# A longer spin, output weights staged in layer two's key buffers, and a new instruction order in a two-layer recurrent-memory transformer kernel

## The chip, the cores and the metric

The kernel runs on one core of one Trainium2 chip. The metric is the device time of one execution in microseconds (us), lower is better; the median of several executions is used. A profiled execution gives, beside its time, the span from its first to its last instruction and a trace of every instruction.

The core's engines work side by side, each through its own queue in order: PE (TensorE, matrix products), PEld (its weight loads), ACT (ScalarE), DVE (VectorE), POOL (GpSimd) and SP, which here mainly issues DMAs. Matrix products write to eight banks of PSUM (psC0, psC1, psG0 to psG5); ACT or DVE then copies the result to SBUF, which is called an eviction below.

## The reference

Two blocks are applied twice to x, a sequence of 2,048 tokens of 448 values. Block A is attention over segments of 32 tokens with a recurrent memory of 8 rows; block B is a gated MLP. Cut to what matters:

```python
def A(x, mem0, Wq, Wk, Wv, Wo):            # 16 heads of 256
    mem = mem0
    for s in range(64):
        h = concatenate([mem, x[32 * s : 32 * s + 32]])       # 8 + 32 rows
        q, k, v = h @ Wq, h @ Wk, h @ Wv                      # per head
        scores = (q @ k.T) / 16     # masked: the 32 rows causally, the 8 memory rows see all
        o = softmax(scores) @ v
        o = o @ Wo                                            # summed over heads
        mem = o[:8]; outs.append(o[8:])
    return concatenate(outs)

def B(x, Wg, Wu, Wd):                       # 448 -> 1792 -> 448
    return (relu(x @ Wg) * (x @ Wu)) @ Wd

x = x + A(layernorm(x));  x = x + B(layernorm(x))
x = x + A(layernorm(x));  x = x + B(layernorm(x))             # the same weights again
```

The memory makes block A a chain: segment s needs the memory rows that segment s - 1 gave.

## The kernel before, in words

**Weights.** The kernel first folds the weights. For each head it makes a product of Wq and Wk (tensor `A`, 16 heads in pairs) and a product of Wv and Wo (tensor `Bsb`), so that a layer needs only `u = h A`, scores `u h^T`, `y = P h` and `o = y B`. `weights()` loads Wq and Wk of four groups of pairs into staging slots `Wst` (which lie in `Bsb`), turns each half by eight transposes on PE (`transposes`, matmuls at L818), evicts them to `WT` (in `glu`), and multiplies (`product`, matmuls at L832). Wv and Wo are staged as well: Wo of eight pairs lies in two pieces of `glu`, three of `P3`, two of `Ug` and one of `GG`. `values(0)` and `values(1)` turn Wv and multiply by Wo into `Bsb`, four pairs each. A buffer that serves as staging is written for its real purpose only when the last product has read it; `s.alias` and the lists `homes` and `held` make these dependences.

**The first loads.** The first group's Wq and Wk come in eight half loads on SP (192 KB each) and four tails of 64 rows on ACT's queue; the other groups in whole loads with tails. All DMAs of SP go out in SP's order.

**The chain.** `chain(step)` does one segment's memory rows for both layers at once; layer two runs `LAG = 7` steps behind layer one. A step goes: u of 16 rows (matmuls at L1008, in two halves), eviction to `Usb`, transposes on DVE (`turn_u`), scores (L1204), softmax, y (L1262, L1265), o against all of `Bsb` (L1047), then a split into a high and a low part, a small product with `Sel`, and copies to `mT`, to `HT` (POOL, L1080) and to `HR`. The first two steps use the unfolded Wv and Wo (`unfused`, L1113 to L1136). `mT` is what the next step starts from.

**The bulk.** `att_group(l, t, g, bo)` does the 32-token rows of tile t (128 tokens) in layer l for a quarter of the heads: u (L1350, two PE steps), scores (L1376), softmax, y, and o (matmuls at L493). `glu_units` and `glu_down` do block B (L1453 for two tiles at once, L1482 for one). Layer norms are in `norm()`.

**Buffers the change touches.** `HT[l][i]` holds the transposed rows of a tile (tokens and memory), `HR[l][i][p]` the same rows as they stand; layer two has three of each (`NB = (2, 3)`). `Ug[0]` and `Ug[1]` hold an attention group's u. A part of `Ug` must be zero, and `values(1)` clears it when Wo has been read from there.

**The order.** All operations are recorded with their dependences in `_Sched`. A planner with fixed costs then sets each engine's order, with one exception: the order of PE is given by hand, as the string `LINE` (which operation comes next, as a place in the list of those left). The string `ORDER` shifts the priority of the units for the other engines. Where the plan has PE idle for over 300 ns, a `filler` is put in (matmuls at L1518 whose result nobody reads). At run time each engine goes through its own list and waits only on semaphores, so PE never overtakes a waiting instruction.

**The spin.** Ahead of everything PE runs matmuls on zeros (L726), to have been busy before the first weights arrive.

**Tilings.** The array is used whole (128x128), or in two tiles of 64x128, two of 128x64, four of 128x32 or eight of 64x32, by the operands' shapes.

Of the kernel before, what the change touches and what calls it, by code (L numbers as in the profile page):

```python
# [12 lines left out]
D = 448  # L13
H = 16
# [4 lines left out]
L = SEG + M  # L19
# [13 lines left out]
ORDER = ("nxaaaaRsTJCzqNVMHniXRBAAODOorIenAPcbGLePMZTGQySGNMXZBDwVyuXhaACIHMfFCXuphjeYMKYtUsaWkfMXtpJaAgHaAbLaADAaaifqaa"  # L33
         "CaErvaIxqaWGwaRkhOaaLuqWkNdgaQuPXZBKEynmeoJu0HfCQl0MwaaatbabtAkiXHsQsZ0dHowILewNSoxIZjcHVaNeDjCfCagAauEXqApt0j"
         "TRxJQkadZnDmoUpHkKAFrefyXxZyAfa0AaCuLCodjnUCwiPsJMumVy0TMpAFSpzPpN0YWHTHGtFqFRlusRAfoMzlZSXZNuHXUKaU0a00bqjuDu"
         "cFNcqkuriahKqgGDnmKHXCPHllFMUmAPOcnzgFaLsaadbMEbHAzMlqUalEZAZizDQgaACUlydMwOKrjOTlLTvA0jvRyfduychiEayenUPAKOBB"
         "IBcapvaNSwmHpHBiFqvwgFrd0XhGXvIpPtWuIbMdReygmGGJvVtwMaAoaNGALx0XHI0UoMSEEkSachUGKI0JuLiFEcwQpAbsmYtqbUupfRABfN"
         "ze0r0rTHlxXSarXfBOaiHaijfdEcucmPIzmyBaNgyigcQXRJEIqSDxNLXsuRdOOfOfYaaO0atzGjqhbmuGEHrcNyUgojwyQYJCiksNHhdXJQcY"
         "YOWSocVtAeQVNmadnRfxwyWGqcEMsNsvHaEQaNUOQV0CqJHn0tGCeaapxJaAVqQfjPuPDDlOg0NsVmlUorZaAwauSIJuThQdIMZFYGMKxZzIwI"
         "nHKpgwgRCWBXCgzBgcavLyLLkxnD0UQjvcZaZpTYcDPwacUQaUKaupymeEQhiBhplfCdH0CDklUQEALrUmDmVsArfamfjdXVEdaIbaOWlzVdxX"  # L40
         "nEHVASIOqaAqoSatDxvHjEEYzRsQNYBuPAUmpEdKtzazNqTDijehyQunEAcKTKYaUYaDrLGdaRoQwDomvQRM0qLDGsTAATkVinpVobRqhEXzxj"
         "laBpawxCrupxDWkqREvPWFqNidrcwvRfUstZMGxybrqmfFiiEmIrJNa0qViFEhYigRZtaKiDaaawaueKaPtCbw0hYXZYrOaaaaaasHrlKxhaaa"
         "aaaaaaaaaaaaaaaauINdINAsaRekmbza")

SIGNS = "ABCDEFGHIJKLMNOPQRSTUVWXYZabcdefghijklmnopqrstuvwxyz0123456789+-*/=<>()[]{}.,:;!"
LINE = ("AEEAAAAAAHDFCCCAABBAIHADBDBBAAAIHBCAACAABAIHCECDCBABAIHHFABCCBAKAHHBFDDCBAAI1IDECBAAAJBAKHCBAABBBAgAgAeACFABAY"
        "PAFVAPTAhAFAQAOAiNAbALAAJABHAZAFBAACXABAAbFBEADPQAECMDAEQKGAAPEPOGEAEDAIDCABBDABAAWAAAKARAAPHdAGSAZAQEAAACLBEP"
        "AEDcc=AFaAAYDDWAVVVAATDACCPPAAAMAAKlKsKAJJAIAHHAAFAADACABBBWBBAMSYAAWeAJbUAIILAVKKAAAEEAHDAbaFFCCWCFAZBSACQABO"
        "OOAOAMAALvLA1KQCJIICHHHAHGGGGAcFAAACHCBAAAAXBAAAMBAYXQAcJUAFIAWGAAABCEPCABBBaaEBADCAETZAARCCPAANNNAALLALL43LRA"
        "rJJCIBHHHAGAIHeAGAACJDCCAAAAABCAATMBAXfWKcKKTAYMfuNAsLAaAAAEEIAiDA65GFPCC0CAEB2wBAubBaBFpppFeFdlAAjkkAAZhfBLkB"  # L50
        "dPbb7AaaaKJCBXWAXWBAUAAAXEQAOOhOOOmPAPNAONMdCBAQJRDWACCjFZFXLFFFIIAQEEIAtsDRHGAnAAGqkLHiGAgggAAeAffAAbACagAAYB"
        "A3VVAAASSSBSArQCBCAONCAKAJAAAGLAFgFFFAHADACPADCSaZBLQBVbBKZBIwBBBAESZAFDACCC)(FpFFCC-(GCC8ABA5WCB222AASzzAAzyW"
        "eQVuAzQhZqgpoCnnnBmConlAAkqAiiAhIAKAAAbbbELcRYEXYYXqFhFcVAAASAEQWFEOOOHOxAANLGFZY65IAAA1AFAy3RDwIEDtttAtFAqArq"
        "DoOENDkGAAJgAf-EDdddGAcAaAbbDDAAAWATAARwRuRlAQQQDDEAAAAJAYeIAAAhgngHTATShEGFE2RAACAKXNB0BKIBBBFIFBERAA//EdDCF8"
        "CC6CAW8A2bBAzzzZAAwAQwwRbirsyAZgGnEmDMkBjjjAjAhBhhgAAekPJCTAAY2YszYYYAaAWBrAUWVC1CSAREWAAOsOUCCMMMtAOEKAAH22CV"
        "UCyAEAEWztPDr~GDDpppGDAmmCmmCDCiAhADAAdCBbfADZZZEDAAVAWWAAATRoRuRWArQECEABBAJJJAJAHAATggZGAREjRFEOeADVAOAYOBuB"
        "1LOBBBLmLBUEB><ACJCC+cCC7ABA4mCC111AA0zA10YAyRWAtbssirQatAoooBonDBmmMAjAiGCBfAeAhIcccAAACYAXZZEiWDBUBTZADAAPWP"
        "GCBMMMAAKCII+9QQ7J*ABA3MF1bAAyyyDyOwAxwDUMCsAxEAPInmEl:DkkkGAAhhAihE4fDAdAEAAZCCXAAAAASSSBAhoEFACBAAAAHAAAETZg"
        "GneSGGRQAACWDABNYBwBIVBBBHxHFBADA)(FhFFPC-H>CAaBA5n4mD222AA0A11AZTAxAW1tAtbr,Rqh]AsoooBnnBAmlCABAIgAAAdIAbHHAA"
        "bXXXCZCGUCWVAAASAPAPUOOFBALLLDUULKA88CHPeH3AGA05AzZAxxxACAuuAvuLBAJqQAABmAFkj:BAhhhD)EDeAdFLAEEaaAAWAAAUAAYSRm"  # L60
        "RkAQQQADCBNCAAJAWDbAAAERcSbiREAAXRABBPOwXvLLBOTKKBnLB00KBBBKQFFFrBADA43~XEeD0C5CCAwBRuAVwRrrrQ~BqASPooECmsckAa"
        "iAhAgggGCKdCfeAAAbhRBXBXBAVUvDtCSSSFARAPAPDCONeAEAUKDImIdIbDOHHHLLIAFFHJOutAAACpDYAmAAkMCBhhhAhDAeHAeeC{BEAYZf"
        "AAXWCVAYATTTAARArQRQAmtWPGANBDBBJAIIIJAAGATAYonSeFRbRGFSAAcVDAgAAAtALzKAAAEJEADA<=gnGF+CHA/B6aA4nEE111AAVzyAzy"
        "AYAvAAt1yssjrrrAaqpBAnNpoAlCCKBALgAlPDdAcbAAfdZZZaHQaXAWYX)FVOUAHbBRWAQF5FOOOPARAMAFVVG6J5TZJaAAQHDOGNNNAAMLAO"
        "NDEIKAAGHAFFAEEEAADCAQBAdGASBGFAINIIDRDJAABBFKAAADCAEADDAAEAAAAABAFBAGFDDDAAB")
# [408 lines left out]
def mm_cost(*ns):  # L474
    return sum(max(n, 54) / 2.4 + 2.5 for n in ns)
# [65 lines left out]
NB = (2, 3)  # L541
NX = 6
NUG = 2
NSH = 3

KZ, KT, KW = 384, 448, 576
# [8 lines left out]
MEM = [("mT", c) for c in range(2)]  # L555
# [13 lines left out]
class _Kernel:  # L569
# [42 lines left out]
    def sb(self, name, shape, dtype=BF):  # L612
        return self.st.enter_context(self.nc.sbuf_tensor(name, shape, dtype))
# [4 lines left out]
    def alloc(self):  # L618
        sb = self.sb
# [37 lines left out]
        self.HT = [[sb(f"HT{l}_{i}", [128, 4, 4, L]) for i in range(NB[l])] for l in range(2)]  # L657
        self.HX = [[sb(f"HX{l}_{i}", [128, 3, 128]) for i in range(NB[l])] for l in range(2)]
        self.HR = [[[sb(f"HR{l}_{i}_{p}", [128, KW]) for p in range(2)] for i in range(NB[l])] for l in range(2)]
# [46 lines left out]
    def constants(self):  # L706
        s = self.s
# [5 lines left out]
        def pool(fn, **k):  # L713
            s.add("pool", 500, lambda E, e: fn(E), **k)
# [5 lines left out]
        hk = [("P3", 2, 0)]  # L720
        s.add("dve", 400, lambda E, e: E.memset(hG[:, 0:576], 0.0), w=hk)
        wb = self.bank("C")

        def spin(E, e):
            for _ in range(9):
                i = E.matmul(wb.ap()[:, 0:D], lhsT=hG[:, 0:128], rhs=hG[:, 128:576], start=True, stop=True)  # L726
            return i
        s.add("pe", 9 * 378, spin, r=hk, w=[wb], alloc=[wb])
# [37 lines left out]
        for l in range(2):  # L766
            for i in range(NB[l]):
                for p in range(2):
                    pool(lambda E, l=l, i=i, p=p: E.memset(self.HR[l][i][p][:, KZ:KW], 0.0),
                         w=[k for h in range(2) for k in (("HRx", l, i, p, h), *(("HRm", l, 4 * i + 2 * p + h, v) for v in range(4)))])  # L770
        for f in rest:
            f()

# [7 lines left out]
    def weights(self):  # L781
        s = self.s
        def load(src, p, slot, halves=(0, 1)):
            if halves != (1,):
                s.part()
            c0 = 512 * p
            if slot < 8:
                a, b = 256 * halves[0], 256 * halves[-1] + 256
                first = len(halves) == 1
                self.dma(self.Wst[slot][:, 0:3, a:b], src[0:384, c0 + a:c0 + b].rearrange("(k p) c -> p k c", p=128), 620 * (b - a),  # L790
                         w=[("Wst", slot, h) for h in halves], prio=0 if first else None, cost=520)
                if halves[0] == 0:
                    self.dma(self.Wst[slot - slot % 2][64 * (slot % 2):64 * (slot % 2) + 64, 3, :], src[384:448, c0:c0 + 512], 53000,
                             w=[("Wst3", slot, h) for h in range(2)], prio=0 if first else None, cost=520, eng="act" if first else "sp")
                return
            self.dma(self.Wst[slot][:, 0:3, :], src[64:448, c0:c0 + 512].rearrange("(k p) c -> p k c", p=128), 393216,
                     r=[("turned", 16)], w=[("Wst", slot)])
            self.dma(self.Wst[slot][0:64, 3, 0:256], src[0:64, c0:c0 + 256], 32768, r=[("turned", 16)], w=[("Wst3", slot)])
            self.dma(self.Wst[slot][64:128, 3, 256:512], src[0:64, c0 + 256:c0 + 512], 32768, r=[("turned", 16)], w=[("Wst4", slot)])
# [70 lines left out]
        self.Wos += [quad(b.rearrange("p a g b -> p (a g b)")[:, 0:4 * D]) for b in self.Ug]  # L870
        homes = [[], []] + [[("P3", i, 0)] for i in range(NSH)]
        homes += [[("Ug", u, k, v) for k in range(3) for v in range(2)] + [("Ug", u, 3, v, hh) for v in range(2) for hh in range(2)] for u in range(2)]
# [20 lines left out]
        def values(part):  # L893
# [13 lines left out]
            if part:  # L907
                for i in range(NUG):
                    s.add("pool", 800, lambda E, e, i=i: E.memset(self.Ug[i][:, 3, :, :], 0.0), w=[("Ug", i, 3, v, hh) for v in range(2) for hh in range(2)])
# [69 lines left out]
    def chain(self, step):  # L979
# [19 lines left out]
        for half in range(2):  # L999
# [11 lines left out]
            s.add("pe", mm_cost(*[D] * 7), fn, r=MEM + [(q, v) for q in MEM for v in range(2)] + ["mTr"] + (["mT3"] if third else []) + self.A_all, w=ub, alloc=ub, room=[("Usb", 2 * half + v) for v in range(2)], mode=4, **P)  # L1011
# [313 lines left out]
    def att_group(self, l, t, g, bo):  # L1325
# [11 lines left out]
        ak = [q for q in self.A_all if q[1] in pairs] + (self.B_all if l + t == 0 and g < 2 else [])  # L1337
# [316 lines left out]
```

## Time and profile before

| | |
|---|---|
| median of 3 runs | 1490.98 us (1489.66 to 1491.23) |
| profiled execution, its own time | 1489.86 us |
| its span | 1487.5 us |
| instructions | 79,091 |
| PE busy | 1473.7 us (99%), 35,063 matmuls |
| DVE busy | 1137.5 us (76%) |
| ACT busy | 922.1 us (62%) |
| POOL busy | 176.4 us (12%) |
| mean granted PE clock | 0.999 |
| DMA | 33.85 MB, mean 23 GB/s; 261 GB/s in the first fortieth of the span |

The profile gives, by engine, busy time, groups of instructions by line and form, and what ended the idle time before them. "L818" is line 818 of the kernel. Matmuls overlap, and the end of each is modelled, so a busy PE isn't the same as a PE at its peak: the spacing of the starts shows how fast it goes.

### The profile page before, as it was taken

Reading aid. Unit: us, or ns where it says so; the run is one execution under the profiler, and the core shown is the slowest. Engines: PE = TensorE matmul, PEld = TensorE weight load, DVE = VectorE, ACT = ScalarE, POOL = GpSimd, SP = SyncE. Lnnn points to the kernel's source line nnn. Section 1 sums busy time; section 2 is a strip of 40 time slices with the busy share of each in tenths; the row PEclk is TensorE's granted clock in tenths of the full one; section 3 lists DMA queues with packets and bytes.
Section 4 is the critical chain, followed back from the end, with each engine's and each line's share of the span. In section 5 each row is a group of like instructions: output and inputs, shape, how many; then the busy total and the mean of one; then the engine's idle time right before and its main releaser. Section 6 shows DMA issues by size and latency. Waiting matters only on the chain.

```text
span 1487.5 us, 79091 instructions
## 1 busy us (share of the span) xinstructions
PE 1473.7 (99%) x35063; PEld 1041.5 (70%) x35063; DVE 1137.5 (76%) x3750; ACT 922.1 (62%) x2650; POOL 176.4 (12%) x684
## 2 busy tenths in 40 slices
PE   9999999999999999999999999999999999999999
PEld 6556767667767776777767767777667776777676
DVE  6657778788878878687877878687786878778865
ACT  6766657666656766566666656566564666565643
POOL 3011111111111111011110111011110111110000
PEclk9999999999999999999999999999999999999999
DMA  9512200000000000000000000000000000000000
GB/s 261 164 26 69 52 8 8 9 9 8 9 4 18 5 8 14 3 17 6 15 7 8 15 8 15 4 18 5 18 4 10 11 12 11 5 11 5 11 5 15
DMA packets 62245, 33.85 MB, mean 23 GB/s; under 512 B 31808, under 2 KB 61776, under 8 KB 61904
## 3 DMA queue, kind: packets, MB, share of 16 engines
q1 hardware_dynamic: 61584, 28.54, 7.5%
q8 instruction: 276, 4.52, 1.3%
q14 instruction: 65, 0.53, 0.1%
q10 hardware_dynamic: 320, 0.26, 0.1%
HBM read 21.36 MB, written 1.84 MB: 16 GB/s over the span
## 4 chain that ended last, share of the span: by engine, by line
PE 96%; DVE 1%; ACT 1%; DMA 1%; issue 0%; SPq 0%; ACTq 0%; POOL 0%
PE psG L493 24%; PE psG L1350 17%; PE psC L1047 11%; PE psG L1453 9%; PE psC L1008 9%; PE psG L1008 5%; PE psG L1262 3%; PE psG L832 3%; PE psG L1482 3%; PE psG L1376 3%; PE psG L1047 2%; PE psC L1262 1%; PE psC L1204 1%; PE psG L818 1%; PE psC L1350 1%; PE psC L493 1%
## 5 line engine op out<-in xcount | busy, mean ns | idle before, releaser
L493 PE MATMUL psG<-Bsb,P 128*128 128x448 bf16 x1344 | 287.4, 352 | 0.0
L1350 PE MATMUL psG<-HT,A 64*128 64x128 bf16 x4776 | 279.9, 216 | 1.2 <-issue 0.7
L1350 PE MATMUL psG<-HX,A 64*128 64x128 bf16 x3582 | 262.2, 216 | 0.0
L1350 PEld LDWEIGHTS psG<-HT,A 64*128 64x128 bf16 x4776 | 230.5, 94 | 11.9 <-issue 4.0
L483 ACT ACTIVATE Ug<-psG 64x128 bf16<-64x128 f32 (+2 forms) x438 | 157.3, 377 | 56.3 <-PE psG L1350 39.0
L1350 PEld LDWEIGHTS psG<-HX,A 64*128 64x128 bf16 x3582 | 190.7, 94 | 0.0
L493 PEld LDWEIGHTS psG<-Bsb,P 128*128 128x128 bf16 x1344 | 116.1, 97 | 97.4 <-issue 9.7
L1047 PE MATMUL psC<-Bsb,YTm 128*32 128x448 bf16 x3192 | 161.6, 353 | 0.2
L1188 DVE STREAM_TRANSPOSE uT<-Usb 128x384 bf16<-128x384 bf16 x280 | 144.4, 536 | 0.0
L1008 PE MATMUL psG<-A,mT 64*32 64x448 bf16 x3948 | 140.6, 350 | 0.0
L1008 PE MATMUL psC<-A,mT 64*32 64x448 bf16 x3892 | 139.4, 350 | 0.1
L1453 PE MATMUL psG<-GG,glu 64*128 64x256 bf16 x2338 | 134.7, 269 | 0.0
L1047 PEld LDWEIGHTS psC<-Bsb,YTm 128*32 128x32 bf16 x3192 | 80.2, 97 | 63.6 <-issue 2.3
L1453 PEld LDWEIGHTS psG<-GG,glu 64*128 64x128 bf16 x2338 | 111.4, 94 | 17.7 <-issue 3.0
L483 ACT ACTIVATE P<-psG 128x448 bf16<-128x448 f32 x226 | 114.3, 545 | 7.0 <-PE psG L1265 4.2
L1008 PEld LDWEIGHTS psC<-A,mT 64*32 64x32 bf16 x3892 | 72.1, 92 | 52.6 <-ACT mT L483 6.6
L486 DVE CAST Ug<-psG 64x128 bf16<-64x128 f32 (+2 forms) x234 | 98.0, 428 | 13.8 <-PE psG L1350 9.0
L493 PE MATMUL psG<-glu,P 128*128 128x448 bf16 x434 | 94.8, 352 | 0.0
L486 DVE CAST P<-psG 128x448 bf16<-128x448 f32 x131 | 79.3, 613 | 12.5 <-PE psG L1265 11.6
L1008 PEld LDWEIGHTS psG<-A,mT 64*32 64x32 bf16 x3948 | 73.9, 92 | 21.3 <-issue 1.0
L1464 DVE TENSOR_TENSOR P<-P,psG 128x512 bf16<-128x512 bf16 x83 | 56.9, 686 | 41.4 <-ACT P L1463 41.0
L1463 ACT ACTIVATE P<-psG 128x512 bf16<-128x512 f32 x84 | 50.0, 595 | 59.5 <-PE psG L1453 51.2
(252 smaller groups left out, 3069.8 us busy)
## 6 DMA issues: line engine op xcount, KB each, us to landing
HR<-xn SPq DMA_DIRECT2D x128, 32.0 KB, 1.9
Tsb<-Rsb SPq DMA_DIRECT2D x256, 1.5 KB
Tsb<-Rsb SPq DMA_DIRECT2D x256, 2.0 KB
Bsb<-in_A_Wq_dram SPq DMA_DIRECT2D x6, 384.0 KB, 6.0
Bsb<-in_A_Wk_dram SPq DMA_DIRECT2D x6, 384.0 KB, 5.5
HR<-Rsb SPq DMA_DIRECT2D x126, 1.5 KB
HR<-Rsb SPq DMA_DIRECT2D x126, 2.0 KB
X<-in_A_x_dram SPq DMA_DIRECT2D x16, 112.0 KB, 3.0
```

Source lines behind the costliest of these rows:

```text
L483: return E.activation(out, i, ACT.Copy, scale=1.0 if scale is None else scale)
L486: return E.tensor_copy(out, i)
L493: return E.matmul(out, lhsT=lhsT, rhs=rhs, **k)
L832: i = E.matmul(bk.ap()[row0:row0 + mn, to:to + of.stop - of.start], lhsT=lhs[:, et, m0:m0 + mn], rhs=rhs[:, et, of], start=(et == 0), stop ...
L1008: i = E.matmul(ub[v].ap()[32 * j:32 * j + 32, 0:D], lhsT=self.mT[rw, WHERE[b], first:first + 32], rhs=cols, start=(b == 0), stop=(b == 6), ...
L1047: x = E.matmul(bo.ap()[32 * j:32 * j + 32, 0:D], lhsT=self.YTm[:, q, :], rhs=self.Bsb[:, chunks[q], :], start=(i == 0), stop=(i == 13), ti ...
L1188: self.s.add("dve", 560, busy=486.0, fn=lambda E, e, v=v, of=of: E.transpose(outs[:, 2 * v:2 * v + 2], of), r=[("Usb", 2 * half + v)], w=[ ...
L1262: return E.matmul(ps[:, n * q:n * q + n], lhsT=HR[rows, 128 * q:128 * q + 128], rhs=PT, start=True, stop=True, tile_position=(b, 0))
L1350: i = E.matmul(ub[v].ap()[:, 128 * n:128 * n + 128], lhsT=self.A[rw, b, a0:a0 + 128], rhs=HT[rw, WHOLE[b], :, 0:SEG] if CROSS[b] is None e ...
L1453: i_ = E.matmul(two[v].ap()[:, 256 * c:256 * c + 256], lhsT=self.Wgu[rw, b, f0:f0 + 128], rhs=self.GG[rw, :, WHOLE[b] if CROSS[b] is None ...
L1463: s.add("act", ev_cost(512)["act"], lambda E, e, dst=dst, z=z: E.activation(dst, z(0), ACT.Relu), r=[two[0]], w=w, room=old)
L1464: s.add("dve", dv_cost(512), lambda E, e, z=z, dst=dst: E.tensor_tensor(dst, dst, z(1), ALU.mult), r=[two[1]], w=w)
```

## The change

Six things change.

1. The spin has 18 matmuls instead of 9, and the planner's cost for it is raised with it.
2. Wo of the two pairs that was staged in `Ug` is now staged in layer two's `HT` and `HR`. For that, `HT` and `HR` become one tensor for each layer, with slices. `Ug` is cleared at the start, and layer two's `HR` padding is cleared behind `values(1)` instead of at the start.
3. The first tile's u steps (groups 0 and 1 of layer one) no longer wait for all of `Bsb`.
4. Each half of the chain's u step waits only for the half of `A` that it reads, not for all of it.
5. The planner reckons with 4,500 ns until the first tails of 64 rows land.
6. `ORDER` and `LINE` are new throughout, so every engine's order differs.

```diff
-            for _ in range(9):
+            for _ in range(18):
                 i = E.matmul(wb.ap()[:, 0:D], lhsT=hG[:, 0:128], rhs=hG[:, 128:576], start=True, stop=True)
...
-        s.add("pe", 9 * 378, spin, r=hk, w=[wb], alloc=[wb])
+        s.add("pe", 9 * 378 + 9 * 189, spin, r=hk, w=[wb], alloc=[wb])
...
-        self.HT = [[sb(f"HT{l}_{i}", [128, 4, 4, L]) for i in range(NB[l])] for l in range(2)]
+        self.HTall = [sb(f"HT{l}", [128, NB[l], 4, 4, L]) for l in range(2)]
+        self.HT = [[T[:, i] for i in range(NB[l])] for l, T in enumerate(self.HTall)]
...
+        self.HRall = [sb(f"HR{l}", [128, NB[l], 2, KW]) for l in range(2)]
+        self.HR = [[[T[:, i, p] for p in range(2)] for i in range(NB[l])] for l, T in enumerate(self.HRall)]
...
+        for i in range(NUG):
+            pool(lambda E, i=i: E.memset(self.Ug[i][:, 3, :, :], 0.0), w=[("Ug", i, 3, v, hh) for v in range(2) for hh in range(2)])
...
-                             w=[("Wst3", slot, h) for h in range(2)], prio=0 if first else None, cost=520, eng="act" if first else "sp")
+                             w=[("Wst3", slot, h) for h in range(2)], prio=0 if first else None, cost=520, eng="act" if first else "sp", land=4500.0 if first else None)
...
-        self.Wos += [quad(b.rearrange("p a g b -> p (a g b)")[:, 0:4 * D]) for b in self.Ug]
+        self.Wos += [quad(b[:, 0:4 * D]) for b in (self.HTall[1].rearrange("p n a g b -> p (n a g b)"), self.HRall[1].rearrange("p n a b -> p (n a b)"))]
...
-                for i in range(NUG):
-                    s.add("pool", 800, lambda E, e, i=i: E.memset(self.Ug[i][:, 3, :, :], 0.0), w=[("Ug", i, 3, v, hh) for v in range(2) for hh in range(2)])
+                s.add("pool", 900, lambda E, e: E.memset(self.HRall[1][:, :, :, KZ:KW], 0.0), w=homes[6])
+                s.add("pool", 300, lambda E, e: E.memset(self.HTall[1][:, 0, 0, 0, 0:8], 0.0), w=homes[5])
...
-            s.add("pe", mm_cost(*[D] * 7), fn, r=MEM + [(q, v) for q in MEM for v in range(2)] + ["mTr"] + (["mT3"] if third else []) + self.A_all, w=ub, alloc=ub, room=[("Usb", 2 * half + v) for v in range(2)], mode=4, **P)
+            s.add("pe", mm_cost(*[D] * 7), fn, r=MEM + [(q, v) for q in MEM for v in range(2)] + ["mTr"] + (["mT3"] if third else []) + [q for q in self.A_all if q[1] % 4 // 2 == half], w=ub, alloc=ub, room=[("Usb", 2 * half + v) for v in range(2)], mode=4, **P)
...
-        ak = [q for q in self.A_all if q[1] in pairs] + (self.B_all if l + t == 0 and g < 2 else [])
+        ak = [q for q in self.A_all if q[1] in pairs]
```

The strings `ORDER` and `LINE` (some 1,150 and 2,200 characters) are replaced as a whole and not shown.

75 lines of the change are left out of this document (37 added, 38 removed).

## The prediction

> **What bounds the kernel now.** I read the page first, then PE's busy time by stretch, then PE's timeline of the first 30 us, where two of the edits lie.
>
> ```profile
> span 1487.5 us, 79091 instructions
> PE 1473.7 (99%) x35063; PEld 1041.5 (70%) x35063; DVE 1137.5 (76%) x3750; ACT 922.1 (62%) x2650; POOL 176.4 (12%) x684
> PE 96%; DVE 1%; ACT 1%; DMA 1%; issue 0%; SPq 0%; ACTq 0%; POOL 0%
> ```
>
> PE is busy for 99% of the span and makes up 96% of the chain that ended last. No other engine is near it. So time can only come from three places: fewer or cheaper PE instructions, fewer changes of the array's tiling, and PE's gaps. The windows say where the gaps are (columns: window, length, PE busy, clock, DMA share, GB/s).
>
> ```profile
> 0.00:12.00 12.00, 8.49 (x67) 0.86 0.88 236
> 12.00:50.00 38.00, 37.85 (x590) 1.00 0.89 268
> 50.00:100.00 50.00, 47.96 (x816) 1.00 0.21 62
> 100.00:200.00 100.00, 98.98 (x2545) 1.00 0.20 52
> 200.00:350.00 150.00, 147.17 (x3895) 1.00 0.05 9
> 350.00:700.00 350.00, 349.66 (x8520) 1.00 0.04 9
> 700.00:1100.00 400.00, 399.42 (x9571) 1.00 0.05 11
> 1100.00:1440.00 340.00, 339.67 (x8112) 1.00 0.04 9
> 1440.00:1487.50 47.50, 44.44 (x1000) 1.00 0.05 13
> ```
>
> Idle are 3.51 us up to 12, 2.04 from 50 to 100, 1.02 and 2.83 to 350, and 1.25 in the 1,090 us to 1440. The 3.06 at the end are the last addition and store behind PE's last matmul; the new order ends in the same interleaved down matmuls of the last two tiles, so they stay. All that can be won from gaps lies in some 9 us of 1,487, most of it before 350 us. A record lasts longer than the spacing of matmuls (below, 0.22 against 0.056 us), so each gap is really some 0.16 us longer than it is shown.
>
> ```profile
> 1.22 3.54 PE L726 MATMUL psC<-P 128*128 128x448 bf16 x9 [1.22 <-DVE cvec L756]
> 6.59 1.07 PE L818 MATMUL psG<-ident,Bsb 128*128 128x128 bf16 x16 [1.83 <-DMA Bsb<-in_A_Wk_dram]
> 8.32 2.74 PE L818 MATMUL psG<-ident,Bsb 128*128 128x128 bf16 x24 [0.46 <-DMA Bsb<-in_A_Wk_dram]
> 11.00 3.21 PE L832 MATMUL psG<-glu 128*64 128x384 bf16 x56
> 14.14 2.41 PE L818 MATMUL psG<-ident,Bsb 128*128 128x128 bf16 x40
> 16.66 2.84 PE L832 MATMUL psG<-glu 128*64 128x448 bf16 x28
> 21.33 2.91 PE L832 MATMUL psG<-glu 128*64 128x384 bf16 x56
> 24.17 1.96 PE L818 MATMUL psG<-ident,Bsb 128*128 128x128 bf16 x32
> 26.06 2.84 PE L832 MATMUL psG<-glu 128*64 128x448 bf16 x28
> ```
>
> Columns are start, length, engine, line, tiles, count and the wait before. 32 transposes from 24.17 to the next product at 26.06: one takes (1.96 - 0.22) / 31 = 0.056 us, 32 take 1.80, and 0.09 us are left over. That is what a change of tiling costs (128x128 to 128x64). At 8.32, 24 transposes take 2.74, which is 0.11 each, twice as long. The clock in narrower windows shows why:
>
> ```profile
> 4.80:8.20 3.40, 1.28 (x22) 1.00 1.12 277
> 8.20:11.60 3.40, 3.28 (x28) 0.51 1.07 307
> 11.60:15.00 3.40, 3.40 (x70) 0.99 1.10 299
> ```
>
> A stretch of 3.4 us in which PE was busy for 1.28 is followed by one at half clock, and that by full clock again. The nine spin matmuls end at about 4.6 and the first weights let PE start at 6.59; the lost half clock costs 24 x 0.053 = 1.3 us on the transposes and some 0.35 on the first products, 1.7 in all.
>
> **The spin, and the first 17 us: -0.6 us.** The 18 matmuls run nine at 0.37 (3.54 us less the tail of the last) and, once the clock is granted, nine at half of that: from 1.22 to about 6.3, just ahead of 6.59. The stretch from 4.8 to 8.2 is then idle for some 1.0 us (0.3 before 6.59, 0.7 behind 7.5) where it was idle for 2.1, and the half clock should go. But the new order gives back part of this. It puts eight transposes of the fifth weight load third, where before they stood fifth, and moves the loads of two x tiles in front of the second group's key weights.
>
> ```profile
> 2.82 0.60 SPq L775 DMA_DIRECT2D Bsb<-in_A_Wq_dram  x1
> 7.97 2.30 SPq L775 DMA_DIRECT2D Bsb<-in_A_Wk_dram  x4
> 12.11 0.96 SPq L775 DMA_DIRECT2D X<-in_A_x_dram  x2
> Bsb<-in_A_Wq_dram SPq DMA_DIRECT2D x4, 192.0 KB, 5.7
> Bsb<-in_A_Wk_dram SPq DMA_DIRECT2D x6, 64.0 KB, 5.5
> X<-in_A_x_dram SPq DMA_DIRECT2D x16, 112.0 KB, 3.0
> ```
>
> The fifth load is issued at 2.82 and lands 5.7 later, at 8.5 (I take 8.7, since PE waited for its fourth until 8.32). PE does two groups of transposes from 6.59 to 7.5 and then waits to 8.7. Five groups of eight follow (40 x 0.056 = 2.2) to 10.9, the 56 products of the first half (24.17 - 21.33 = 2.84, with the change of tiling) to 13.8, and a group to 14.25. The next needs the tail of the key weights, second of the four at 7.97, so issued near 8.6 and landed near 14.1. Now 2 x 112 KB at 268 GB/s stand in front, 0.86 us, so it comes at 15.0. Two groups more and the change of tiling end at 16.0, and PE has done what it had done at 16.66 before: 0.6 us won. Bounds: -1.7 if no load waits; +1.3 if the clock is granted so late that all 18 run slowly (18 x 0.37 from 1.22 ends at 7.9, 1.3 after 6.59). I take -0.6, the value from the landing rows.
>
> [...]
>
> **Changes of tiling: -1.2 us.** I counted PE's instructions in both orders. The work is the same, matmul for matmul, but for 9 more in the spin and 8 fillers where there were 12. Neighbours with different tilings are 555 where they were 568. 13 x 0.09 = 1.2. Bounds: 0, where a change fell into a wait anyhow, to -1.4, at 0.11.
>
> **Fillers: 0.** Ten of 448 columns and two small ones become eight of 448. They sit where PE would wait, so their going wins nothing by itself.
>
> **The output weights in the key buffers, and the released first tile: 0.** The bytes and the DMAs are the same. Of 192 score-weight steps (L1350's, two per group) only one comes in front of the end of the output products, so the freedom is hardly used; its worth is in the next part. The memsets behind the products change on POOL:
>
> ```profile
> L909 POOL MEMSET Ug<- x2: 526/528/529, 98.6 to 101.5; 128x512 bf16 x2
> 109.63 0.21 POOL L1080 COPY HT<-mT 128x32 bf16<-128x32 bf16 x1 [7.63 <-DVE mT L1070]
> ```
>
> Two of 0.53 us for 512 elements become one of 1,152 elements, about 1.2 us, and one of 8. They wait for the last products, and behind them POOL has the chain's HT copy, which waited another 7.63 us: that idle time hides them. Without the cover it would be 0.3 us once. The two moved to the start stand behind memsets that POOL finishes by 17, and the chain begins near 50.
>
> **Waits of the new order: -2.1 us.** Every stretch has a new PE order. For each of the 2,170 PE steps I added up the PE work that stands between it and the last PE step it needs through another engine, at the spacings above, and took off the evictions between, at durations like these:
>
> ```profile
> L483 ACT ACTIVATE P<-psG 128x448 bf16<-128x448 f32 x226 | 114.3, 545 | 7.0 <-PE psG L1265 4.2
> L486 DVE CAST P<-psG 128x448 bf16<-128x448 f32 x131 | 79.3, 613 | 12.5 <-PE psG L1265 11.6
> PE psG L832 <- ACT Bsb L483: 1.4, 6, 0.3
> PE psG L1376 <- POOL HT L1080: 0.5, 2, 0.3
> ```
>
> The last two rows are what such a step costs: 1.4 us in 6 waits, 0.5 in 2, so 0.24 each as shown. Behind the first 20 us, 32 steps of the old order are short of cover by over 0.2 us, and 26 of the new: 6 x 0.24 = 1.44. Short by less are 51 and 43; at a third of that price (they stall only when the engine in between is late, too) 8 x 0.08 = 0.64. Together -2.1. Most of it is between 50 and 100 us (13 far-short steps become 8), where 2.04 us are idle. Bounds: -5.9, which is all the idle time from 50 to 350, and +4, if 28 steps more than counted, a third of the 83, are late because ACT and DVE take their evictions in another order (28 x 0.15).
>
> **The sum.** -0.6 - 1.2 - 2.1 = -3.9. Against the profiled execution's 1489.86 (span 1487.5 and 2.4 around it) that gives 1486.0; that execution lies at the lower end of the runs, whose median is 1490.98, and against the median it gives 1487.1. I say 1487.0.
>
> **The rivals.** About 0.2% (3.0 us) is what a measurement of this kernel can tell from no change.
>
> First, only what is certain comes through: the changes of tiling, 1.2 us, while the first 17 us are bound by the loads and the count of short steps means nothing. 1490.98 - 1.2 = 1489.8. For it: DMA is busy at 236 to 268 GB/s through the first 50 us. Against it: after 11 us no PE row of the timeline shows a wait for a DMA. 0.16.
>
> Second, the clock is granted late. If the grant can fall anywhere against the start, the spin runs slowly to 7.9, and the start costs +1.3 in place of -0.6: 1489.0. [...] This case's trace has one start only, with the grant somewhere before 6.6. 0.08.
>
> Third, slower: the chain's steps come late in the steady part. Some 53 of its steps lie between 350 and 1440, where PE is idle for 1.25 us in all. If the new order leaves the chain's evictions or POOL's HT copy late by 0.13 us in each step, that is +7, and with the 3.0 that the rest brings, near 1494. It decides from 0.11 us a step on. For it: every engine's order is new in this part too, and a wait on that HT copy is among the rows above. Against it: in this part short steps fall from 17 to 13. 0.08.
>
> **How the numbers follow.** The forecast, faster by 3.9, has 0.68, of which a part lies near the line of 1488.0. The two small cases have 0.24 and the slow one 0.08. Some of the forecast's own spread falls within 0.2%, some of the small cases beyond it; these cancel. So faster 0.67, same 0.24, slower 0.09. The range: the lower end takes -5.9 for the waits with -1.2 and -1.7 (1482.2); the upper end takes in both small cases and a little slip in the steady part, 1491.5, and leaves out the slow case.
>
> **What would show it.** Right: the spin in about 5.1 us, all transposes 0.056 apart, no window at 0.5 between 8.2 and 11.6; one wait for the fifth load to about 8.7 and one for key weights near 14.5; idle PE from 50 to 350 us down from 5.9 to about 4; the steady part as idle as now. Wrong: a window at half clock behind the first transposes, waits for loads through 20 to 45 us, or idle PE above 3 us between 350 and 1440.

## The result, and the profile after

The changed kernel takes 1482.43 us (median of 6 runs, 1481.78 to 1483.46), the kernel before, on the same chip, 1490.8 (1489.66 to 1491.23): a ratio of 0.9946, 95% interval 0.9933 to 0.9959. That is 8.4 us, where 3.9 were forecast. The two profiled executions took 1483.32 and 1489.86, so 6.5 us of it can be looked for in the traces: 6.1 within their spans, and 0.4 outside (2.4 us before, 1.9 after).

From the page of the changed kernel:

```profile
span 1481.4 us, 79079 instructions
...
PE 1470.8 (99%) x35068; PEld 1040.5 (70%) x35068; DVE 1136.3 (77%) x3743; ACT 925.1 (62%) x2659; POOL 176.0 (12%) x678
...
q8 instruction: 276, 4.52, 1.3%
...
PE 97%; DVE 1%; ACT 1%; issue 0%; DMA 0%; POOL 0%; SPq 0%
```

PE is still the bound, with 2.9 us less busy time and 3.2 us less idle time in its span. (The third line, a queue by packets, MB and share, is used further down.) PE's busy time in the same stretches as before:

```profile
0.00:12.00 12.00, 10.66 (x98) 1.00 0.88 236
12.00:50.00 38.00, 37.72 (x604) 1.00 0.91 259
50.00:100.00 50.00, 48.53 (x811) 1.00 0.22 69
100.00:200.00 100.00, 99.08 (x2547) 1.00 0.19 52
200.00:350.00 150.00, 148.04 (x3950) 1.00 0.05 9
350.00:700.00 350.00, 349.05 (x8490) 1.00 0.04 9
700.00:1100.00 400.00, 399.48 (x9648) 1.00 0.05 11
1100.00:1440.00 340.00, 339.82 (x8185) 1.00 0.04 9
```

Idle time from 50 to 350 us fell from 5.89 to 4.35 us; from 350 to 1440 it is 1.65 us instead of 1.25. The start, in PE's timeline and in the windows of 3.4 us:

```profile
1.22 6.38 PE L728 MATMUL psC<-P 128*128 128x448 bf16 x18 [1.22 <-DVE cvec L758]
...
7.52 0.61 PE L821 MATMUL psG<-ident,Bsb 128*128 128x128 bf16 x8
...
7.99 2.84 PE L821 MATMUL psG<-ident,Bsb 128*128 128x128 bf16 x48
10.94 2.91 PE L835 MATMUL psG<-glu 128*64 128x384 bf16 x56
...
15.29 2.84 PE L835 MATMUL psG<-glu 128*64 128x448 bf16 x28
```
```profile
4.80:8.20 3.40, 3.40 (x25) 1.00 1.06 278
8.20:11.60 3.40, 3.29 (x60) 1.00 1.14 307
```

None of these windows is at half clock and the transposes are 0.056 us apart. The spin took 6.38 us: its first 16 matmuls start 0.37 us apart, the last two 0.27 and 0.19 behind the one before (the trace's first record of the clock, at full, begins at 6.94; the clock column shows 1.00 also for the time before it, of which there is no record). The transposes still end where they were forecast, at 10.9. The second half's products start at 15.29, where they started at 16.66: 1.4 us won. I call this start the mark below. Behind it, the last matmul but one starts 1462.6 us later instead of 1467.3: 4.7 us won.

### The profile page after: what moved, and what is told of

It reads as the page before. It is cut to its first block, busy times and chain, and to the rows that moved or that the text cites. A ratio compares the mean times of both kernels' runs of the same rounds, so it can differ in the third digit from the quotient of the medians.

```text
span 1481.4 us, 79079 instructions
## 1 busy us (share of the span) xinstructions
PE 1470.8 (99%) x35068; PEld 1040.5 (70%) x35068; DVE 1136.3 (77%) x3743; ACT 925.1 (62%) x2659; POOL 176.0 (12%) x678
## 3 DMA queue, kind: packets, MB, share of 16 engines
q8 instruction: 276, 4.52, 1.3%
## 4 chain that ended last, share of the span: by engine, by line
PE 97%; DVE 1%; ACT 1%; issue 0%; DMA 0%; POOL 0%; SPq 0%
PE psG L493 24%; PE psG L1354 17%; PE psC L1051 12%; PE psC L1012 9%; PE psG L1457 9%; PE psG L1012 4%; PE psG L835 3%; PE psG L1266 3%; PE psG L1486 3%; PE psG L1380 3%; PE psC L493 2%; PE psC L1208 1%; PE psC L1266 1%; PE psG L821 1%; PE psG L1051 1%; PE psG L1269 1%
## 5 line engine op out<-in xcount | busy, mean ns | idle before, releaser
L493 PE MATMUL psG<-Bsb,P 128*128 128x448 bf16 x1288 | 276.2, 353 | 0.0
L1051 PE MATMUL psC<-Bsb,YTm 128*32 128x448 bf16 x3528 | 178.8, 353 | 0.4
L1012 PE MATMUL psC<-A,mT 64*32 64x448 bf16 x3920 | 152.8, 350 | 0.2
L1012 PE MATMUL psG<-A,mT 64*32 64x448 bf16 x3920 | 152.1, 350 | 0.0
L1051 PEld LDWEIGHTS psC<-Bsb,YTm 128*32 128x32 bf16 x3528 | 88.7, 97 | 70.8 <-issue 2.5
L486 DVE CAST Ug<-psG 64x128 bf16<-64x128 f32 (+2 forms) x260 | 107.6, 424 | 15.5 <-PE psG L1354 10.7
L1012 PEld LDWEIGHTS psC<-A,mT 64*32 64x32 bf16 x3920 | 78.7, 92 | 57.2 <-ACT mT L483 5.2
L483 ACT ACTIVATE P<-psG 128x448 bf16<-128x448 f32 x210 | 106.4, 545 | 8.6 <-PE psG L1269 7.1
L486 DVE CAST P<-psG 128x448 bf16<-128x448 f32 x148 | 89.1, 614 | 12.7 <-PE psG L1269 11.2
L1058 DVE TENSOR_TENSOR Olo<-psC,Ohi 128x448 bf16<-128x448 f32 x65 | 40.4, 622 | 64.3 <-ACT Ohi L1057 63.8
```

The costliest lines, as they stand in the source:

```text
L483: return E.activation(out, i, ACT.Copy, scale=1.0 if scale is None else scale)
L486: return E.tensor_copy(out, i)
L493: return E.matmul(out, lhsT=lhsT, rhs=rhs, **k)
L1012: i = E.matmul(ub[v].ap()[32 * j:32 * j + 32, 0:D], lhsT=self.mT[rw, WHERE[b], first:first + 32], rhs=cols, start=(b == 0), stop=(b == 6), ...
L1051: x = E.matmul(bo.ap()[32 * j:32 * j + 32, 0:D], lhsT=self.YTm[:, q, :], rhs=self.Bsb[:, chunks[q], :], start=(i == 0), stop=(i == 13), ti ...
```

## The experiments

**The chips.** Each ratio below is against runs of the kernel before on the same chip: e1 to e4 ran on one, f1 and f2 on a second, g1 to g3 on a third, h1 to h3 on a fourth, where the kernel before has medians of 1489.9, 1488.9, 1488.6 and 1489.2 us. The changed kernel as it is ran only for the result and in e4, so f, g and h have no run of it beside them.

**What the table holds.** For every profiled execution I split the time from the mark to the start of the last matmul but one into three parts, from the start times of all its matmuls. Changes of tiling count 0.096 us each: that much later than with the same tiling does a step start behind a change (in the traces of before and after, four matmuls of 448 columns are followed after 0.285 instead of 0.189 us). "Inside" is the time from the first to the last matmul of a step, summed over all steps. "Between" is the rest, from one step's last matmul to the next step's first, waits included.

| execution | mark | behind it | changes | between | inside |
|---|---|---|---|---|---|
| before | 16.66 | 1467.3 | 54.2 | 217.8 | 1195.2 |
| e3, staging, old order | 14.48 | 1466.8 | 54.2 | 217.3 | 1195.2 |
| g3, before shifted by 58 | 14.33 | 1470.0 | 54.2 | 217.3 | 1198.4 |
| h3, before shifted by 93 | 15.18 | 1470.0 | 54.2 | 220.0 | 1195.7 |
| e1, long spin, old order | 15.96 | 1471.3 | 54.2 | 218.4 | 1198.7 |
| after | 15.29 | 1462.6 | 53.0 | 216.8 | 1192.8 |
| e4, after again | 15.33 | 1462.9 | 53.0 | 215.8 | 1194.0 |
| e2, short spin, new order | 16.48 | 1464.6 | 53.0 | 216.6 | 1195.0 |
| h1, after shifted by 29 | 14.63 | 1465.9 | 53.0 | 217.8 | 1195.1 |
| g2, after shifted by 58 | 15.57 | 1464.1 | 53.0 | 217.1 | 1194.0 |
| h2, after shifted by 93 | 15.39 | 1465.1 | 53.0 | 218.1 | 1194.0 |
| f1, more tilings | 15.35 | 1469.9 | 57.0 | 217.9 | 1194.9 |
| f2, more short steps | 15.04 | 1484.6 | 53.0 | 237.9 | 1193.7 |
| g1, more just covered | 15.72 | 1468.3 | 53.0 | 225.4 | 1189.9 |

Traces of one order differ among themselves: in the old one (e1 aside) by 2.7 us between steps and 3.2 inside, in the new one by 2.3 and 2.3.

**e1: the long spin alone, in the old order.**

```diff
-            for _ in range(9):
+            for _ in range(18):
```

> The kernel before with one edit: 18 spin matmuls instead of 9, every engine's order as before. Theory (the gain is spread: fewer waits and tilings in the new order, about 1 us at the start): the window at half clock between 8.2 and 11.6 us goes, the first products start near 10.1 instead of 11.0 and run at full speed, 1.5 us are won and nothing else changes: 1489.3 us against 1490.8. Rival (the gain is mostly the clock at the start, since the medians lie 8.4 us apart where the two profiled executions lie 6.5 apart): 1486.8 or less.

Measured: 1492.17 us, ratio 1.0014 (1.0004 to 1.0024): slower by 0.14%, where the theory had 1489.3 and the rival 1486.8 or less. Both miss. Its timeline, and windows around 130 us:

```profile
1.22 6.50 PE L726 MATMUL psC<-P 128*128 128x448 bf16 x18 [1.22 <-DVE cvec L756]
7.56 1.06 PE L818 MATMUL psG<-ident,Bsb 128*128 128x128 bf16 x16
...
132.55 0.23 PE L1350 MATMUL psG<-HT,A 64*128 64x128 bf16 x2 [1.97 <-issue]
```

```profile
130.10:133.50 3.40, 1.43 (x52) 1.00 0.20 58
133.50:136.90 3.40, 3.40 (x23) 0.50 0.23 63
```

In the old order the spin's end, near 7.5, sets the start of the transposes, which the loads alone would have allowed at 6.59, and in other executions near 5. Far from the start there is something else in this execution: PE stops for 1.97 us inside a step, waiting for nothing that the profile shows, and the next 3.4 us are at half clock.

The mean granted clock tells which runs had such a stretch: the four traces with 0.999 hold one window of 3.4 us at half, the ten with 1.000 none. Of e1's 12 runs seven have 0.999 and average 1493.3 us; the five with 1.000 average 1491.0, and that is still 1.4 more than the kernel before in its 19 runs with 1.000 on this chip (1489.6). So part of e1's loss is lost clock, and the rest fits its late start: its mark lies at 15.96, those of e3, g3 and h3 at 14.3 to 15.2. Why the clock is lost more often here is not shown.

**e2: the new order with the short spin.**

```diff
-            for _ in range(18):
+            for _ in range(9):
```

> The changed kernel with 9 spin matmuls instead of 18, every engine's order as in the changed kernel. Theory: the half clock comes back behind the fifth load, 40 transposes take some 1.4 us more, 1483.9 us against 1482.4. Rival (mostly the clock): 1486.5 or more.

Measured: 1484.74, ratio 0.9964 (0.9949 to 0.9979), 1.2 us more than e4 on the same chip.

```profile
6.14 0.61 PE L821 MATMUL psG<-ident,Bsb 128*128 128x128 bf16 x8
8.42 3.85 PE L821 MATMUL psG<-ident,Bsb 128*128 128x128 bf16 x40 [1.68 <-DMA Bsb<-in_A_Wq_dram]
```
```profile
4.80:8.20 3.40, 1.34 (x20) 0.98 1.07 286
8.20:11.60 3.40, 3.18 (x31) 0.52 1.13 316
```

Here the gap and the half clock are back, and the mark comes 1.2 us later. Six of the eight runs have a mean clock below 1.000, none of the 11 runs of the changed kernel (result and e4). So spin and order belong together: the new order waits for the fifth load third, and the spin fills part of that wait. Without the long spin the new order still wins 5.2 us against the kernel before on this chip.

**e3: staging in the key buffers, u not held, half of A, but the old order and spin.** (Item 5, the planner's 4,500 ns, is left out here and was not tried alone. Two of the edited places:)

```diff
-        self.Wos += [quad(b.rearrange("p a g b -> p (a g b)")[:, 0:4 * D]) for b in self.Ug]
+        self.Wos += [quad(b[:, 0:4 * D]) for b in (self.HTall[1].rearrange("p n a g b -> p (n a g b)"), self.HRall[1].rearrange("p n a b -> p (n a b)"))]
...
-        ak = [q for q in self.A_all if q[1] in pairs] + (self.B_all if l + t == 0 and g < 2 else [])
+        ak = [q for q in self.A_all if q[1] in pairs]
```

> The kernel before with the staging in layer two's key and row buffers, the first tile not held for the output products, and each half of the chain's u step waiting for its own half of A; 9 spin matmuls, the planner's constants and both order strings as before. In the order the tilings stay 568, the steps far short of cover 32 and those short by less 50. Theory: these edits win nothing without a new order, 1490.8 us within 0.7. Rival (the released buffers and steps fill PE's gaps between 50 and 100 us): 1488.5 or less.

Measured: 1489.51, ratio 1.000 (0.999 to 1.001). These edits alone give nothing beyond the interval, some 1.5 us to either side. What they do give is room: the new order puts the first u step of the bulk at place 120 of 2,167 on PE, ahead of output products for which it would have to wait with the old staging or the old hold. In the traces PE stands at a step that waits, and so do the steps behind it (in e2 PE is idle for 1.68 us up to 8.42, waiting for the fifth load). So the new order can't exist without these edits.

**e4: the changed kernel again.** No edit.

> The changed kernel as it is, on the same chip as the other three and with a second profile. Theory: 1482.4 us within 0.7; the gaps behind 20 us as in its first profile, and the start differs with the moment at which the full clock is granted. Rival (the order's waits vary from one execution to the next and the difference is partly luck): gaps behind 20 us that differ by over 1 us in sum from the first profile.

Measured: 1483.55, ratio 0.9956 (0.9941 to 0.9971), a little outside the 0.7 us of the theory. Behind the mark it differs from the first trace by 0.25 us, but that is the sum of 1.0 less between steps and 1.2 more inside.

**f1 and f2: the prices of the prediction, one at a time.** Both move PE steps of the changed kernel by a few places, by `LINE` alone. In f1, for example, the first two steps moved are a y step of one group (L1418, tiles of 64x128) and an o step of the chain (L1051, 128x32), which come in turn instead of each kind together.

```diff
-        "sJJCIBHHHAHGAHHeAGADAJDCCAAAAABCAATMBAXWeKcLKTAYMveAtALbKAAAEEAjHTA65GuGCI0C5ABxwAveeFkEqqqIApAAmAEEkkAAAhBmBX"
+        "sJJCIBHHHAHGAHHeAGADAJDCCAAAAABCAATMBAXWeKcLKTAYMveAtALbKAAAEEAjHTA65GuGCI0C5ABxAvveeFkEqqqIApAAmAEEkkAAAhBmBX"
...
```

> The changed kernel with 81 PE steps behind 108 us moved by at most four places, so that neighbouring PE instructions with different tilings are 597 instead of 555, while the steps short of cover stay as they were (far short 26 instead of 24, just covered as before; 11 filler matmuls instead of 8). Theory (a change of tiling lies on PE's path and costs 0.09 us each, as the prediction priced it): 42 x 0.09 = +3.8, and 2 x 0.24 and 3 fillers add up to 1.0, so 3.8 to 4.8 above the changed kernel's 1482.4 to 1483.6, that is 1486 to 1488, a ratio of 0.997 to 0.998 to the kernel before, with no more idle PE than the changed kernel shows. Rival (a change of tiling hides in the waits and the weight loads, and the changed kernel is faster for other reasons): no more than 1 us above the changed kernel, 1482 to 1484, ratio 0.995.

```diff
-        "mRkAQQQCEABCAAJEAWAbAAgTeTlTGAUZAAEDRzayQBMCQLLrCKRBB2K0KBBBAEuPAHDDA44E~XECCCUyCCA1vXAtVsssRQ~CqAPoppBDuPmDAk"
+        "mRkAQQQCEABCAAJEAWAbAAgTeTlTGAUZAADDRzayQBMCQLLrCKRBB2K0KBBBAEuPAHDDA44E~XECCCUyCCA1vXAtVsssRQ~CqAPoppBDuPmDAk"
...
```

> The changed kernel with 148 PE steps behind 71 us moved by at most six places, so that 60 PE steps instead of 24 are short of cover by over 0.2 us by the count that the prediction used, at the same 555 changes of tiling (13 filler matmuls instead of 8). Theory (a far-short step costs PE about 0.24 us, as the prediction priced it): 36 x 0.24 = +8.6, and 5 fillers at 0.19 at most 0.9 more, so 1491 to 1493, above the kernel before (ratio 1.000 to 1.002). A second form of it (each such step waits as long as it is short, which sums to +11.7 when a wait also covers the steps behind it): 1495 to 1496, ratio 1.003. Rival (ACT and DVE have slack and the order matters little; the changed kernel is faster for other reasons): within 1 us of the changed kernel, 1482 to 1484, ratio 0.995.

Measured: f1 1490.51, ratio 1.0006 (0.9997 to 1.0015); f2 1504.79, ratio 1.0104 (1.0091 to 1.0118). Both miss, on the far side: f1 costs 7 to 8 us against the changed kernel, f2 some 22. The table counts f1's 42 more changes at 0.096 us, 4.0 in all, and since the time between steps does not fall for it, they did not hide in waits: the price holds. 1.6 more lie between steps, where the count saw 2 far-short steps, and about 1.5 inside; traces of one order differ by as much. In f2 the 36 steps cost 21.6 us between steps, 0.6 each if all of it is theirs, and not 0.24. Its waits, with engine and line waited for, then us in total, times and longest:

```profile
PE psG L513 <- DVE Pm L1226: 2.0, 1, 2.0
...
PE psG L1208 <- DVE uT L1192: 1.4, 1, 1.4
PE psG L1051 <- ACT YTm L483: 1.4, 2, 1.0
PE psG L1380 <- POOL HT L1084: 1.3, 5, 0.4
PE psG L1266 <- ACT PTm L483: 1.3, 2, 0.8
```

Single waits are 1 to 2 us long, where a step was less than 1 us short on paper. The longest, of 1.96 us, ends at 319.35; the scores that it goes back to were done by 316.9. DVE was busy for 5.08 of the 5.30 us from 314.3 to 319.6, and its first row for these scores had to stand behind an eviction of something else:

```profile
316.36 1.15 DVE L486 CAST P<-psG 128x448 bf16<-128x448 f32 x2
317.42 0.23 DVE L1219 TENSOR_REDUCE stm<-psC 128x2 f32<-128x80 f32 x1
...
319.06 0.24 DVE L1226 TENSOR_SCALAR Pm<-Tm,stm 128x40 bf16<-128x40 f32 x1
```

The window with this wait, in which PE was busy for 1.44 of 3.40 us, was followed by one at half clock (0.50), so that a part of f2's loss is half clock and not waiting:

```profile
316.20:319.60 3.40, 1.44 (x50) 1.00 0.04 6
319.60:323.00 3.40, 3.40 (x68) 0.50 0.01 2
```

**g1: steps that the count holds for covered.** Again `LINE` alone, with 208 steps moved. (Of the diffs of f1, f2 and g1 one line of the string each is shown.)

```diff
-        "DeAXAWCBATTTAASRASRxQoQAlEAEMALBAAIIIAIDGAUAAYDmmEQbQaQEEAdAVCAN4AAuAKzKAAAEEAsDGA//hGFC9<HdAB5GA3mE111AAzA00A"
+        "DeAXAWCBATTTAASRASRxQoQAlEAEMALBAAIIIAIDGAUAAYDmmEQbQaQEEAdAPUCA4AAuAKzKAAAEEAsDGA//hGFC9<HdAB5GA3mE111AAzA00A"
...
```

> The changed kernel with 208 PE steps behind 119 us moved by at most seven places, so that the steps that are covered by less than 0.2 us are 194 instead of 135, while the steps short of cover (24 far, 30 by less) and the changes of tiling (555) stay as they were; 11 filler matmuls at most instead of 8. Theory of the prediction (only steps short of cover cost PE time; those just covered cost nothing): within 0.6 us of the changed kernel, 1482 to 1484, ratio 0.995. Second theory (a step's cover is only what lies between two PE steps on paper; ACT and DVE are late with their evictions when these come in bunches, so that the kernel's own plan, which queues all engines, is the better count; that plan gets longer by 10.0 us here, and it got longer by 6.6 and 21.6 in the last two experiments, where 7 and 22 were measured): 1491 to 1494, ratio 1.000 to 1.002, with the added waits of PE on ACT, DVE or POOL at steps that the count holds for covered.

Measured: 1491.13, ratio 1.0015 (1.0007 to 1.0024), 7.6 to 8.7 us above the changed kernel: the second theory. Between steps it loses 9.1 us, near the 10.0 by which the kernel's own plan grows (for f2 they were 21.6 and 21.6; for f1, changes included, 5.6 and 6.6).

```profile
PE psC L1208 <- DVE uT L1192: 1.3, 5, 0.3
```

```profile
1.22 5.16 PE L728 MATMUL psC<-P 128*128 128x448 bf16 x18 [1.22 <-DVE cvec L758]
...
8.92 2.41 PE L821 MATMUL psG<-ident,Bsb 128*128 128x128 bf16 x40 [1.27 <-DMA Bsb<-in_A_Wq_dram]
```

The first of these fences, from PE's waits, has five steps of the chain's scores that wait for DVE's transposes; in the changed kernel's waits that line does not occur. The second, from the timeline, shows the start as it was forecast, since the spin was shorter in this execution: 18 matmuls in 5.16 us, about what nine at 0.37 and nine at 0.19 take, and a wait for the fifth load, here to 8.92.

**g2, g3, h1, h2, h3: the place of the work in PE's stream.** The stop of e1 has smaller sisters in every trace. The first rows come from the kernel before, the second from the changed kernel, the third from g2; each time first the window up to the stop, with the count of PE's matmuls behind the x, then the first row behind the stop.

```profile
0.00:480.40 480.40, 470.86 (x11138) 1.00 0.18 50
480.60 0.21 PE L1350 MATMUL psG<-HT,A 64*128 64x128 bf16 x1 [0.17 <-issue]
```
```profile
0.00:476.60 476.60, 470.42 (x11138) 1.00 0.19 50
477.14 0.21 PE L1354 MATMUL psG<-HT,A 64*128 64x128 bf16 x1 [0.74 <-issue]
```
```profile
0.00:475.60 475.60, 468.22 (x11139) 1.00 0.19 50
476.00 0.23 PE L1356 MATMUL psG<-HT,A 64*128 64x128 bf16 x2 [0.49 <-issue]
```

PE stops behind the 11,138th matmul in two different orders, and behind the 11,139th where all work stands 58 matmuls later. The edit of g2; the others have other numbers in the two loops:

```diff
-            for _ in range(18):
+            for _ in range(12):
                 i = E.matmul(wb.ap()[:, 0:D], lhsT=hG[:, 0:128], rhs=hG[:, 128:576], start=True, stop=True)
+            for _ in range(64):
+                i = E.matmul(wb.ap()[:, 0:32], lhsT=hG[:, 0:128], rhs=hG[:, 128:160], start=True, stop=True)
```

> The changed kernel with 12 of its 18 spin matmuls and 64 of 32 columns behind them, so that all later work stands 58 matmuls later in PE's instruction stream; the order is the same. In the traces so far PE stops inside a step, with no semaphore to wait for, at the same numbers of its stream in each kernel: at the matmuls 2367, 7197, 7326, 11011, 11138 and others, apart by multiples of 127, for 0.2 to 1.0 us each. Theory (the stops belong to the place in the stream, a block of some 127 matmuls with their weight loads): they stay at 2367, 7197 to 7326, 11011 and 11138, which is work that came 58 matmuls earlier in the changed kernel. Rival (they belong to the work): they move to 2425, 7255, 7384, 11069 and 11196. On time: if the order of the work sets how much the stops cost, their sum stays at 2.3 to 3.0 us and the time at 1482 to 1484 (ratio 0.995); if it is where the blocks happen to begin, it may come to the 4 to 5 us of the kernel before, and the time to 1485 (0.997).

> The kernel before with 3 of its 9 spin matmuls and 64 of 32 columns behind them, so that all later work stands 58 matmuls later in PE's instruction stream; the order is the same. Theory (stops belong to the place in the stream): they stay near the matmuls 7069, 7197, 7323, 11138 and 15713. If the order of the work sets their cost, their sum stays at 4 to 5 us and the time at the kernel before's (ratio 1.000); if it is where the blocks begin, it falls to 2 to 3 us and the time by some 2 us (ratio 0.9985).

> The changed kernel with 14 spin matmuls and 33 of 32 columns behind them: all later work stands 29 matmuls later in PE's stream, the order is the same. With 58 the time rose to 1485.6, though the stops added only 0.7 us to the trace and the start 0.3. Theory (the place of the work in the stream is worth some 3 us to the changed kernel, since its stops fall on other work): this one lies anywhere from 1482 to 1487, and differs by over 1.5 us from either the unshifted kernel or the next one. Rival (58 was slower for its start alone, where PE waited 0.66 us for loads): 1482 to 1484 (ratio 0.995), as its spin is nearly the changed kernel's.

> The changed kernel with 10 spin matmuls and 101 of 32 columns behind them: all later work stands 93 matmuls later in PE's stream, the order is the same. Theory (place in the stream matters): 1482 to 1487, differing by over 1.5 us from one of its sisters; the stop at 11138 stays within two matmuls of that number. Rival (the start): with few wide matmuls the start is like that of the shift by 58, 1485 to 1486 (ratio 0.998).

> The kernel before with 1 spin matmul and 101 of 32 columns behind it: all later work stands 93 matmuls later in PE's stream. Theory (place in the stream matters): over 1.5 us from the kernel before, to either side (ratio under 0.999 or over 1.001). Rival (the place costs nothing, as the shift by 58 gave 1.000): ratio 1.000.

Measured:

| kernel | us | ratio to before |
|---|---|---|
| g2, changed, shifted by 58 | 1485.60 | 0.9978 (0.9970 to 0.9987) |
| h1, changed, shifted by 29 | 1485.65 | 0.9973 (0.9963 to 0.9983) |
| h2, changed, shifted by 93 | 1485.10 | 0.9968 (0.9956 to 0.9980) |
| g3, before, shifted by 58 | 1489.68 | 1.0000 (0.9991 to 1.0008) |
| h3, before, shifted by 93 | 1489.13 | 1.0003 (0.9994 to 1.0013) |

The stops stay at their numbers in the stream, in g2 (3131, 11012, 11139) and in g3 (7070, 7197, 7324, 11139): the first theory. A number does not bring a stop in every execution: in h1, h2 and h3 there is none of over 0.12 us at 11138, where h2 was expected to have one. On time the answer is mixed. The kernel before doesn't care for the shift, so h3's theory fell. The changed kernel is 1.6 to 3.2 us slower with each of the three shifts, all alike. h1 contradicts the start as the cause: its mark is the earliest of all the changed ones and it is no faster. But shifted and unshifted were not run side by side on one chip. Against the kernel before on the same chip the changed kernel wins 8.4 and 6.4 us unshifted and 3.5, 3.0 and 4.1 us shifted (by 29, 58 and 93), and the intervals of e4 and h2 overlap. So whether the place in the stream or the chip makes this difference is open; no run settles it. In the traces the shifted ones have about 1.3 us more between steps and 1.0 more inside. Compared at the same shift and on the same chip, changed against before, the change is worth 4.1 us (58) and 4.0 us (93) by the medians, 3.3 and 4.7 by the means.

## Why the prediction was right, and where not

**The sign and the bound** were right: PE stayed the bound and the new order is what wins. Without the long spin it wins 5.2 us (e2), while the long spin alone (e1) and the other edits without the order (e3) win nothing. The order of PE and that of the other engines, and the planner's new constant, were not tried apart. The size was 3.9 forecast, 8.4 measured, and 6.4 the second time (e4, with 1489.9 for the kernel before on its chip). Of the reasons given, the tilings hold, the start holds on the profiled pair alone, and the waits hold in part.

**The first 17 us (-0.6).** In the profiled pair they gave -1.4. The half clock is gone, as forecast. The two forecast waits, for the fifth load and for key weights near 14.5, do not show: PE began its transposes at 7.5 in place of 6.59 and then found its loads landed. But one trace of the kernel before was a narrow base, and its half clock is the exception: of the 88 runs of the kernel before on the four chips of the experiments only nine have a mean clock of 0.999. The price was right (on the chip of e1 to e4 six runs with 0.999 have a median of 1491.35 us, 19 with 1.000 one of 1489.74); it was only rarely paid. The mark lies at 14.3 to 16.7 in the four executions of the old order with the short spin, and at 14.6 to 16.5 in the six of the new order. On average the start wins nothing that these traces can show. How many of the result's own runs of the kernel before had the half clock is not on record, so that part of its 8.4 may be that. The late grant, a rival with 0.08, did come in the changed kernel's execution (a spin of 6.38 us instead of 5.16, the first record of the full clock at 6.94 where the kernel before has it at 4.84) and cost nothing: with the early grant (g1) PE waits for the fifth load to 8.92 and ends its transposes later, at 11.4.

**Changes of tiling (-1.2).** Right: 0.096 us each where 0.09 was taken, 1.25 for 13.

**Fillers and staging (0).** Staging is right: e3 is 1.000. The fillers were not tried alone.

**Waits (-2.1).** This term was mis-sized, and its method fell. Between steps the six traces of the new order lie 1.1 us below the four of the old in the mean (217.0 against 218.1; e1 is left out for its half clock), and the two groups overlap. What is clear of that is the class itself. A recount with the planner's own costs finds 23 steps short by over 0.2 us before and 19 after (the prediction's count had 32 and 26, that of the later expectations 24 for the new order); in the four traces of the old order they lose 3.6 to 3.9 us beyond the usual spacing, in the six of the new one 3.0 to 3.1. So 0.8 us of the 2.1 shows in every trace. But the price of 0.24 does not carry over: it is 0.16 to 0.17 for these steps, 0.6 in f2, and steps that the count calls covered can cost 9 us (g1). The step that failed is the reckoning of cover for each step by itself, with evictions at their own duration. It leaves out that an eviction can stand behind other work of ACT or DVE, as in f2, where DVE was busy for 5.08 of the 5.30 us around the longest wait. The kernel's own plan, which has the queues of these engines, gets 3.2 us shorter behind the mark by the change, where tilings and waits together gave 2.3.

**What had no term.** Inside steps the new order takes 2.0 us less in the mean of its six traces (1194.2 against 1196.2), and 2.4 in the profiled pair. Most of this is stops like the one at 11138, as far as they can be told apart. As traces of one order differ by up to 3.2 us in this, it isn't shown that the order is the cause. Outside the span some 0.4 us less is spent in every run of the changed kernel, and why is open. The profiled pair's 6.5 us are thus about 1.4 for the start, 1.2 for tilings, 1.0 between steps, 2.4 inside and 0.4 outside the span; up to 8.4 the rest is that the profiled execution of the kernel before lies 0.9 us below its median and that of the changed kernel 0.9 above. Averaged over the ten traces, the last matmul but one starts 4.0 us earlier: +0.3 for the mark, -1.25 for tilings, -1.1 between steps and -2.0 inside. So that the forecast sum of 3.9 meets the 4 us of the shifted pairs is in part luck: about half of it came for the reasons given.

## What to carry to other kernels

This order couldn't be priced step by step. Moving 208 steps by at most seven places, which the count held for harmless, cost 7.6 to 8.7 us (g1), as much as the whole change brings; the kernel's own plan, which queues ACT and DVE, gave 10.0. So here the cover of a PE step has to be reckoned with these queues. The 18 spin matmuls instead of 9 lost 2.3 us in the old order (e1) and won 1.2 in the new one (e4 against e2), where a wait for a load stands behind it (1.68 us in e2), so a spin is chosen together with the order of the loads. A half clock seen in one trace, which nine of 88 runs had here, is checked against the mean clock of many runs before it is counted as a gain. And a result of a few us in a long kernel is checked by shifting its instruction stream, on one chip: here 4 us stayed of 6.4 to 8.4.

## What the hardware showed unexpectedly

PE stops inside steps, with no semaphore, at certain numbers of its instruction stream: 2367, 7197, 11138 and others, about 127 matmuls apart or a multiple of it. In the traces of before and after eleven such stops leave PE idle for 0.13 to 0.74 us each, in e1 one for 1.97. The page's instruction queue (above) moved 276 packets with 4.52 MB, 16.4 KB each; 35,068 matmuls and as many weight loads are 254 to a packet, 127 of each. That the stops have to do with these packets is my guess from the two numbers; no run shows it. Over 14 profiled executions, a place on this grid of 127 before which 254 matmuls went by in under 7.5 us was followed by a stop of over 0.12 us in 20% of 370 cases, any other in 2% of 3,452. All such stops add up to roughly 1 to 8 us in one execution.

The clock fell to half behind windows in which PE was busy for 1.28 to 1.44 us of 3.41. In the trace of the kernel before, the records of the clock run from 4.84 to 8.25 at full, from 8.25 to 11.66 at half, and then at full: 3.41 us each for the first two. In steps of this length, counted from the first record of the full clock in each trace, PE was busy for 1.28 us in the window before the one at half in the kernel before, and for 1.44 in e2, in e1 (at 130 us, with the stop of 1.97) and in f2 (with the wait of 1.96). Behind windows with 1.82 (g3) and 1.69 (h3) it did not fall; no run shows what happens between 1.44 and 1.69. In h3:

```profile
4.87:8.28 3.41, 1.69 (x30) 1.00 1.00 288
8.28:11.69 3.41, 3.23 (x62) 1.00 1.13 310
```
